# VectorE sums in place of a third matmul in 114 of 384 first-layer units, with in-place squares and later lags

## The chip, the cores and the metric

One core of a Trainium2 chip. The metric is the device time of one execution, in microseconds, as the median over several executions. All executions quoted here ran in the fast state; the time before the change varied from 652.4 to 655.0 us over all its runs. Ratios are the mean time of one kernel's fast runs over that of the other's of the same rounds, so not quite the ratio of the medians that are quoted.

Engine names in the profile: PE is TensorE, PEld its weight loads, DVE is VectorE, ACT is ScalarE, POOL is GpSimd. Two memories occur in the code: SBUF holds the kernel's tiles, and PSUM takes the results of matmuls. A *bank* is here one PSUM tile of 128 x 512 fp32 values; the kernel keeps six that the transforms and the first layer share, and two for the second layer. The *granted clock* is the share of TensorE's full clock that the profile records.

## The reference, cut to what matters

```python
# x: (8, 3008, 256), w_in: (256, 2048), w_out: (2048, 256), all float32
X = np.fft.fft(np.fft.fft(x, axis=1), axis=2).real
X = X.reshape(24064, 256)
h = np.maximum(X @ w_in, 0.0)
out = h * h @ w_out
```

The kernel computes the sequence transform as four real transforms per sequence, folds the transform along the features into the first layer's weights, and uses the symmetry of the result. Rows k and S-k of the output ("a pair") share their transforms: one is a sum, the other a difference of the same products. There are 8 x 1505 = 12040 pairs.

## The kernel before: the parts that the change touches

Pairs are worked in 25 chunks, mostly of 512 pairs. A *unit* is one chunk times 128 of the 2048 hidden features, so a full chunk has 16 units. The main loop takes one unit per *step*. With P and Q the transformed data of a sequence, and G1, G2 the folded weights, a unit needs

- relu(G1 P + G2 Q) for rows k ("s half"),
- relu(G1 P - G2 Q + an edge term) for rows S-k ("d half").

The kernel before makes both in one PSUM bank, with three matmuls of 512 columns. G3 is -2 G2, but 0 in the edge row (the last of Q's 128 rows), which enters both halves with the same sign.

```python
    def x_front(c, u):                       # two matmuls, relu of the s half
        ...
            for sn, G in ((0, G1), (1, G2)):
                for (b, i, o, l) in segs:
                    mm(xb[:, j, o : o + l], G[:, fs], PQ[b][sn][:, i : i + l], ...)
        act(r_of(c, u, 0), xb, AF.Relu)                          # L575
        return (c, u, xb)

    def x_back(cur):                         # third matmul, relu of the d half
        ...
                mm(xb[:, j, o : o + l], G3[:, fs], PQ[b][1][:, i : i + l], False, True)
        act(r_of(c, u, 1)[:, :, ::-1], xb, AF.Relu)              # L585

    def x_square(cur):                       # once per two units
        ...
            vt(h2, r, r, op=ALU.mult)                            # L599
```

The second layer of a chunk (128 matmuls of 256 columns, with 128x128 blocks of h as weights) is spread over the steps of the next chunk. This loop sets the order in which every engine gets its instructions:

```python
    for si, (c, u) in enumerate(steps):
        left = NFC // chunks[c][2] - u
        take = [mmq.pop(0) for _ in range(-(-len(mmq) // left))]   # second-layer matmuls
        cur = x_front(c, u)
        h = len(take) // 2
        posts = [f() for f in take[:h]]
        if prev is not None:
            x_back(prev)
        posts += [f() for f in take[h:]]
        ...
        if prev is not None:
            x_square(prev)
            if prev[0] != c:
                mmq += mm2_ops(prev[0])
        prev = cur
        for f in side.get(si, []):           # transforms of later sequences
            f()
```

So the third matmul of a unit comes one step after its first two, and the square in the same step as the relu that it needs.

## Time and profile before

| | before |
|---|---|
| median of 3 runs | 654.32 us (652.42 to 654.83) |
| profiled span | 651.9 us |
| TensorE, ACT, VectorE busy | 629.8, 511.7, 355.5 us |
| a full chunk, start to start | about 24.4 us, or 25 to 28 with transforms |

The head of the profile page (span, then busy time, share of the span and number of instructions of each engine), and the two lines of its chain of waits:

```profile
span 651.9 us, 11930 instructions
...
PE 629.8 (97%) x4834; PEld 459.5 (70%) x4834; DVE 355.5 (55%) x518; ACT 511.7 (78%) x934; POOL 49.4 (8%) x66
...
PE 92%; DVE 4%; DMA 1%; ACT 1%; issue 0%; POOL 0%; DVEq 0%; ACTq 0%; POOLq 0%
PE po L72 50%; PE xb L72 36%; PE pf L72 6%; DMA x<-in_x_dram,idx 1%; DVE h L599 1%; DVE u L329 1%; DVE wout L660 0%; DVE v L341 0%; ACT r L585 0%; ACT r L575 0%; DVE tm L235 0%; DVE qt L422 0%; ACT os L533 0%; DVE tt L182 0%; ACT G L308 0%
```

The chain says who is to be made shorter: TensorE, with the second layer (po) and the first (xb). Busy time alone would not say so, since matmuls overlap and their ends are modelled. TensorE's rate is read from start to start in the timeline of the kernel before (start, duration, engine, line, operation, output and inputs):

```profile
433.33 0.38 PE L72 MATMUL xb<-pt,G 128*128 128x512 f16 x1
433.55 0.38 PE L72 MATMUL xb<-qt,G 128*128 128x512 f16 x1
433.76 0.60 PE L72 MATMUL po<-wout,h 128*128 128x256 f16 x4
434.20 0.38 PE L72 MATMUL xb<-qt,G 128*128 128x512 f16 x1
```

A matmul "takes" 0.38 us, but the next one starts 0.22 us later; four of 256 columns take 0.44 us. One engine lies idle a great deal, as the waits list of the kernel before shows (who waited for whom: total us, times, longest):

```profile
DVE h L599 <- ACT r L585: 250.8, 164, 3.5
...
PE po L72 <- DVE h L599: 3.5, 2, 2.4
...
PE xb L72 <- ACT r L575: 2.5, 4, 0.9
```

VectorE's squares wait 250 us for ACT's relus, and nobody minds: TensorE waits for a square twice. These waits tell where there is room for more work. What an instruction costs is in the groups by shape of the kernel before (count | busy us, mean ns | idle before and its releaser):

```profile
L599 DVE TENSOR_TENSOR h<-r 128x2048 f16<-128x2048 f16 x184 | 225.2, 1224 | 250.8 <-ACT r L585 250.8
L585 ACT ACTIVATE r<-xb 128x512 f16<-128x512 f32 x368 | 222.0, 603 | 17.2 <-PE xb L72 1.3
...
L329 DVE TENSOR_TENSOR u<-x 127x765 f16<-127x765 f32 x32 | 29.0, 948 | 0.3 <-DMA x<-in_x_dram,idx 0.3
...
L425 DVE TENSOR_TENSOR pt<-as,pf 128x377 f16<-128x377 f32 x8 | 4.4, 548 | 4.1 <-PE pf L72 4.0
```

### The profile page before, as it was taken

The page shows a single profiled execution, that of the slowest core. Times are in us where ns is not written, and L with a number is a line of the kernel's source. Part 1 is how long each engine was busy: PE and PEld are TensorE (multiplying, and loading weights), DVE is VectorE, ACT ScalarE, POOL GpSimd, SP SyncE. Part 2 cuts the span into 40 slices and gives each one's busy share as a digit, 9 for nine tenths or more (in the row PEclk, how much of TensorE's full clock was granted, in tenths as well). Part 3 has the DMA queues.
Part 4 walks back from the last instruction along what each step waited for, and adds up shares of the span by engine and source line. Part 5 has one row for each costly group of instructions (what it writes and reads, how often), then busy time and mean ns, then how long its engine had stood idle before and what let it go on. Part 6 is the DMA issues. An engine that isn't in the chain of part 4 may idle for free.

```text
span 651.9 us, 11930 instructions
## 1 busy us (share of the span) xinstructions
PE 629.8 (97%) x4834; PEld 459.5 (70%) x4834; DVE 355.5 (55%) x518; ACT 511.7 (78%) x934; POOL 49.4 (8%) x66
## 2 busy tenths in 40 slices
PE   3889999999999999999999999999999999999997
PEld 1566677666776777767777668777787677877786
DVE  8878787694764447544674444444334444434331
ACT  5867888777888788788887778887887878888872
POOL 8103023030200004000000000000000000000000
PEclk9989999999999999999999999999999999999999
DMA  8935484572641018111111111111111110111112
GB/s 274 298 85 131 110 210 124 159 180 97 158 115 50 33 44 217 57 38 50 33 49 33 49 34 40 42 45 39 49 34 49 33 49 33 50 37 46 49 50 67
DMA packets 33758, 54.47 MB, mean 84 GB/s; under 512 B 4446, under 2 KB 28562, under 8 KB 33702
## 3 DMA queue, kind: packets, MB, share of 16 engines
q0 software_dynamic: 6256, 27.45, 16.0%
q1 hardware_dynamic: 27398, 26.22, 12.4%
q8 instruction: 38, 0.62, 0.4%
q14 instruction: 18, 0.15, 0.1%
q10 hardware_dynamic: 48, 0.02, 0.0%
HBM read 29.02 MB, written 24.64 MB: 82 GB/s over the span
## 4 chain that ended last, share of the span: by engine, by line
PE 92%; DVE 4%; DMA 1%; ACT 1%; issue 0%; POOL 0%; DVEq 0%; ACTq 0%; POOLq 0%
PE po L72 50%; PE xb L72 36%; PE pf L72 6%; DMA x<-in_x_dram,idx 1%; DVE h L599 1%; DVE u L329 1%; DVE wout L660 0%; DVE v L341 0%; ACT r L585 0%; ACT r L575 0%; DVE tm L235 0%; DVE qt L422 0%; ACT os L533 0%; DVE tt L182 0%; ACT G L308 0%
## 5 line engine op out<-in xcount | busy, mean ns | idle before, releaser
L72 PE MATMUL po<-wout,h 128*128 128x256 f16 x3024 | 445.7, 273 | 3.5 <-DVE h L599 3.5
L72 PEld LDWEIGHTS <-h 128*128 128x128 f16 x3024 | 286.0, 98 | 122.3 <-DVE h L599 4.4
L599 DVE TENSOR_TENSOR h<-r 128x2048 f16<-128x2048 f16 x184 | 225.2, 1224 | 250.8 <-ACT r L585 250.8
L575 ACT ACTIVATE r<-xb 128x512 f16<-128x512 f32 (+1 forms) x384 | 227.8, 593 | 91.2 <-PE xb L72 88.6
L72 PE MATMUL xb<-qt,G 128*128 128x512 f16 (+16 forms) x1024 | 286.5, 323 | 3.8 <-ACT r L575 2.5
L585 ACT ACTIVATE r<-xb 128x512 f16<-128x512 f32 (+1 forms) x384 | 228.2, 594 | 19.0 <-PE xb L72 2.5
L72 PEld LDWEIGHTS <-G 128*128 128x128 f16 x1536 | 144.5, 98 | 41.7 <-issue 7.4
L72 PE MATMUL xb<-pt,G 128*128 128x512 f16 (+16 forms) x512 | 146.8, 324 | 0.0
L533 ACT ACTIVATE os<-po 128x512 f32<-128x512 f32 x94 | 55.7, 592 | 6.3 <-PE po L72 6.2
L329 DVE TENSOR_TENSOR u<-x 127x765 f16<-127x765 f32 x32 | 29.0, 948 | 0.3 <-DMA x<-in_x_dram,idx 0.3
L100 POOL DMA_INDIRECT x<-in_x_dram,idx x18 | 25.0, 1389 | 5.4 <-issue 4.8
L72 PEld LDWEIGHTS <-w 127*128 127x128 f16 (+1 forms) x192 | 21.5, 118 | 5.3 <-DVE w L347 1.0
L393 ACT ACTIVATE as<-pf 128x377 f32<-128x377 f32 (+5 forms) x32 | 15.5, 484 | 9.8 <-PE pf L72 9.7
L123 POOL DMA_DIRECT2D x<-in_x_dram x14 | 7.9, 562 | 198.3 <-DVE u L333 198.1
L72 PE MATMUL pf<-sinT,w 127*127 127x377 f16 (+1 forms) x96 | 20.7, 323 | 0.0
L72 PE MATMUL pf<-cosT,w 127*128 127x377 f16 (+1 forms) x96 | 20.0, 323 | 0.1
L347 DVE TENSOR_TENSOR w<-v 127x381 f16<-127x381 f16 x64 | 19.7, 353 | 0.0
L72 PE MATMUL warm<-ez 128*128 128x512 f16 x18 | 6.3, 520 | 10.9 <-DVE ez L622 10.9
L341 DVE TENSOR_TENSOR v<-u 127x768 f16<-127x768 f16 x32 | 16.5, 552 | 0.3
L72 PEld LDWEIGHTS <-ez 127*128 127x128 f16 (+1 forms) x42 | 4.5, 110 | 15.2 <-DVE ez L622 10.9
L603 DVE TENSOR_TENSOR h<-r 128x528 f16<-128x528 f16 (+2 forms) x24 | 7.5, 339 | 11.2 <-ACT r L585 9.3
L425 DVE TENSOR_TENSOR pt<-as,pf 128x377 f16<-128x377 f32 (+1 forms) x16 | 8.8, 549 | 8.6 <-PE pf L72 7.5
(95 smaller groups left out, 123.6 us busy)
## 6 DMA issues: line engine op xcount, KB each, us to landing
out_dram<-os SPq DMA_DIRECT2D x157, 128.0 KB
x<-in_x_dram POOLq DMA_DIRECT2D x14, 756.0 KB, 10.1
wst<-in_moe_w_in_dram POOLq DMA_DIRECT2D x4, 512.0 KB, 6.6
wot<-in_moe_w_out_dram POOLq DMA_DIRECT2D x1, 2048.0 KB, 14.4
x<-in_x_dram SPq DMA_DIRECT2D x2, 756.0 KB
x<-in_x_dram,idx POOLq DMA_INDIRECT x18, 11.5
x<-in_x_dram POOLq DMA_DIRECT2D x14, 2.0 KB, 12.1
out_dram<-os SPq DMA_DIRECT2D x2, 108.0 KB
```

Of the source, the lines that this page charges most:

```text
L72: nc.tensor.matmul(o, l, r, start=start, stop=stop, skip_group_check=True)
L100: nc.gpsimd.indirect_dma_start(out=x4[0:NP, 2 + s, q : q + rows, :].rearrange("p q d -> p (q d)"), out_offset=None, in_=bass.AP(tensor=x.t ...
L123: nc.gpsimd.dma_start(out=x4[0:NP, s, :, :], in_=up(b, s))
L329: return lambda: vt(u[k, s, q0 : q0 + NQ // 2, 1:D], x4[k, s, q0 : q0 + NQ // 2, 1:D], x4[k, 3 - s, ::-1, :][:, q0 : q0 + NQ // 2, D - 1 : ...
L341: vt(vs[s][k, qs, :], u[k, 0, qs, :], u[k, 1, qs, :], op=ALU.subtract if s else ALU.add)
L347: return lambda: vt(w[k, i, q : q + 3, 0 : P - 1], vs[s][k, q : q + 3, 1:P], vs[s][k, q : q + 3, D - 1 : P : -1], op=ALU.add if i < 2 else ...
L393: act(st["a"][0:m, :], st[0][0:m, :], AF.Copy, bias=0.0, scale=1.0 if fin[0] is None else fin[0])
L425: vt(lo_, a, bp, op=ALU.add)
L533: act(os_, po, AF.Copy, bias=0.0, scale=HS * HS)
L575: act(r_of(c, u, 0), xb, AF.Relu)
L585: act(r_of(c, u, 1)[:, :, ::-1], xb, AF.Relu)
L599: vt(h2, r, r, op=ALU.mult)
```

## The change

The intent: TensorE binds and VectorE idles, so let VectorE make the sum and the difference. In a *split unit* G2 Q and G1 P go to two banks of their own (two matmuls, not three); ACT copies the first to SBUF; VectorE computes 2 g e - G2 Q (e is the edge row of Q, broadcast to all partitions, and g its weights) and then both clamped sums, which are the relus. 114 of the 384 units are split: 2 of 16 in chunks 3 to 5, 5 of 16 in chunks 6 to 14, 7 of 16 in chunks 15 to 23.

Further: relus write straight into the tile that the second layer reads and are squared in place, in a ring of 19 tiles of two units; one of eight squares of chunks 6 to 23 goes to ACT; back matmuls come two steps after the front (LAG), squares one step later still (SQ), and the second layer of a chunk starts at step 3 of the next chunk instead of step 1. The plans for folding later inputs are stretched, and two weight loads are cut in four to fit the ring. The diff, cut to its core:

```diff
+    YZ = [(0, 0)] * 3 + [(2, 0)] * 3 + [(5, 1)] * 9 + [(7, 1)] * 9 + [(0, 0)]
+    # y of 16 units split, z of 8 squares on ACT; u is split where (u * y + 8) % 16 < y
...
-    rp = ctx.enter_context(tc.tile_pool(name="rp", bufs=3))
-    h2p = ctx.enter_context(tc.tile_pool(name="h2p", bufs=2))
+    h2p = ctx.enter_context(tc.tile_pool(name="h2p", bufs=19))
...
+    def e_spread(c):     # the edge row, broadcast to all partitions; issued three steps ahead
+        ...
+            nc.gpsimd.dma_start(out=ebc[c][:, o : o + l], in_=PQ[b][1][P - 1 : P, ...])
+    def x_split(c, u):
+        xs = [psx.tile([P, 512], F32, name=nm, tag="x")[:, 0:n] for nm in ("xo", "xe")]
+        for t, G, sn in ((xs[0], G2, 1), (xs[1], G1, 0)):
+            for (b, i, o, l) in segs:
+                mm(t[:, o : o + l], G[:, fs], PQ[b][sn][:, i : i + l], o == 0, True)
+        bs = tgp.tile([P, 2, CH], F32, name="bs", tag=("tt", "tm")[nsplit[0] % 2])
+        act(bs[0], xs[0], AF.Copy, bias=0.0, scale=1.0)                                # L629
+        def add():
+            stt(out=bs[1], in0=ebc[c][:, 0:n], scalar=gE2[:, u : u + 1], in1=bs[0],
+                op0=ALU.mult, op1=ALU.subtract)                                        # L632
+            def sat(o, t):
+                nc.vector._custom_dve(TENSOR_ADD_SAT, out=o, in0=xs[1], in1=t, s0=BIG, s1=0.0)  # L636
+            sat(r_s(c, u)[:, 0, :], bs[0])
+            relu_d(c, u, lambda o, i: sat(o[:, 0, :], bs[1]))
+        return (c, u, None, add)
...
+        if u // 2 in PLAN[c][1]:
+            act(h2[:, 0:nf], h2[:, 0:nf], AF.Square)                                   # L660
+            rest.append(lambda: act(h2[:, nf:], h2[:, nf:], AF.Square))                # L661
             return
+        vt(h2, h2, h2, op=ALU.mult)                                                    # L663
...
+    LAG = 2
+    SQ = 1
     for si, (c, u) in enumerate(steps):
+        while wait:                          # chunks whose last square was in an earlier step
+            d = wait.pop(0)
+            mmq += mm2_ops(d)
+            due = si + NFC // chunks[d + 1][2]
...
+        flight.append((x_split if u in PLAN[c][0] else x_front)(c, u))
...
+        if len(flight) > LAG:
+            x_back(flight[0])
+            made.append(flight.pop(0))
...
+        if len(made) > SQ:
+            retire()                         # square; after a chunk's last: wait.append(chunk)
+        if len(flight) > 1 and flight[-2][3]:
+            flight[-2][3]()                  # VectorE's sums of the unit of the step before
```

In the changed kernel the relu of the s half is L605 and that of the d half L651.

More of the change, by code (lines that the diff above doesn't have):

```diff
@@ L8 @@
 from concourse._compat import with_exitstack
+from concourse.dve_ops import TENSOR_ADD_SAT
 F32 = mybir.dt.float32
@@ L19 @@
 R23 = float(2.0 ** 23)
+BIG = 3.0e38
 @with_exitstack
@@ L133 @@
     wout16 = const.tile([P, NFC, D], F16, name="wout16")
-    wst = h2p.tile([P, 2, F], F32, name="wst", tag="h2")
-    wot = h2p.tile([P, NFC, D], F32, name="wot", tag="h2")
+    wst = [h2p.tile([P, 2, F // 4], F32, name="wst", tag="h2") for _ in range(4)]
+    wot = [h2p.tile([P, NFC // 4, D], F32, name="wot", tag="h2") for _ in range(4)]
     wS = 2.0 * math.pi / S
@@ L296, in gcast @@
     def gcast(c, cp):
-        cp(win16(c), wst[:, :, c * 512 : (c + 1) * 512])
+        cp(win16(c), wst[c])
     def gmat(c):
@@ L480, with plan, e_weights, e_double @@
         g += n
-    h2t = {}
-    def h2v(c):
-        n = chunks[c][1]
-        return h2t[c][:, 0 : NFC * 2 * n].rearrange("p (f t) -> p f t", f=NFC)
+    YZ = [(0, 0)] * 3 + [(2, 0)] * 3 + [(5, 1)] * 9 + [(7, 1)] * 9 + [(0, 0)]
+    def plan(c, y, z):
+        if chunks[c][1] != CH:
+            return (), ()
+        return ([u for u in range(NFC) if (u * y + 8) % NFC < y],
+                [p for p in range(NFC // 2) if (p * z + 4) % (NFC // 2) < z])
+    PLAN = [plan(c, *YZ[c]) for c in range(len(chunks))]
+    gE = const.tile([P, NFC], F16, name="gE")
+    gE2 = const.tile([P, NFC], F32, name="gE2")
+    def e_weights():
+        for f in range(NFC):
+            nc.sync.dma_start(out=gE[:, f : f + 1], in_=G2[P - 1 : P, f * P : (f + 1) * P])
+    def e_double():
+        ts(out=gE2, in0=gE, scalar1=2.0, scalar2=None, op0=ALU.mult)
+    h2t = {}
+    def h2v(c, u):
+        n, nf = chunks[c][1:3]
+        if (c, u // 2) not in h2t:
+            t = h2p.tile([P, 4 * CH], F16, name="h2", tag="h2")
+            h2t[c, u // 2] = t[:, 0 : 4 * nf * n].rearrange("p (f t) -> p f t", f=2 * nf)
+        return h2t[c, u // 2]
     def mm2_ops(c):
@@ L544, in f @@
                 w = 2 * m if s == 2 else m
-                mm(st["o"][0:w, j, :], h2v(c)[:, fc, o : o + w], wout16[:, fc, :],
+                mm(st["o"][0:w, j, :], h2v(c, fc // nf)[:, fc % (2 * nf), o : o + w], wout16[:, fc, :],
                    fc == 0 and j == 0, fc == NFC - 1)
@@ L553, in mm2_ops, with relu_d, r_s @@
         return ops
-    rt = {}
-    def r_of(c, u, s):
-        g0, n, nf, segs = chunks[c]
-        if u % 2 == 0 and s == 0:
-            t = rp.tile([P, 4 * CH], F16, name="r", tag="r")
-            rt[c, u // 2] = t[:, 0 : 4 * nf * n].rearrange("p (f s n) -> p f s n", f=2 * nf, s=2)
-        o = u % 2 * nf
-        return rt[c, u // 2][:, o : o + nf, s, :]
+    def relu_d(c, u, put):
+        n, nf = chunks[c][1:3]
+        o = u % 2 * nf
+        d = h2v(c, u)[:, o : o + nf, n : 2 * n]
+        k = n % P
+        if k:
+            put(d[:, :, 0:k][:, :, ::-1], slice(0, k))
+            put(d[:, :, k:n][:, :, ::-1], slice(k, n))
+        else:
+            put(d[:, :, ::-1], slice(0, n))
+    def r_s(c, u):
+        n, nf = chunks[c][1:3]
+        o = u % 2 * nf
+        return h2v(c, u)[:, o : o + nf, 0:n]
     def x_front(c, u):
@@ L574, in x_front @@
                        j == 0 and sn == 0 and o == 0, sn == 1)
-        act(r_of(c, u, 0), xb, AF.Relu)
-        return (c, u, xb)
+        act(r_s(c, u), xb, AF.Relu)
+        return (c, u, xb, None)
+    ebc = {}
+    def e_spread(c):
+        g0, n, nf, segs = chunks[c]
+        ebc[c] = esp.tile([P, CH], F16, name="eb", tag="eb", bufs=2)
+        for (b, i, o, l) in segs:
+            nc.gpsimd.dma_start(out=ebc[c][:, o : o + l],
+                              in_=PQ[b][1][P - 1 : P, i : i + l].unsqueeze(1).to_broadcast([1, P, l]))
+    nsplit = [0]
+    def x_split(c, u):
+        g0, n, nf, segs = chunks[c]
+        fs = slice(u * P, (u + 1) * P)
+        xs = [psx.tile([P, 512], F32, name=nm, tag="x")[:, 0:n] for nm in ("xo", "xe")]
+        for t, G, sn in ((xs[0], G2, 1), (xs[1], G1, 0)):
+            for (b, i, o, l) in segs:
+                mm(t[:, o : o + l], G[:, fs], PQ[b][sn][:, i : i + l], o == 0, True)
+        nsplit[0] += 1
+        bs = tgp.tile([P, 2, CH], F32, name="bs", tag=("tt", "tm")[nsplit[0] % 2])
+        bs = [bs[:, j, 0:n] for j in range(2)]
+        act(bs[0], xs[0], AF.Copy, bias=0.0, scale=1.0)
+        def add():
+            stt(out=bs[1], in0=ebc[c][:, 0:n], scalar=gE2[:, u : u + 1], in1=bs[0], op0=ALU.mult,
+                op1=ALU.subtract)
+            def sat(o, t):
[3 more added lines that the diff above has]
+        return (c, u, None, add)
     def x_back(cur):
-        c, u, xb = cur
+        c, u, xb = cur[:3]
+        if xb is None:
+            return
         g0, n, nf, segs = chunks[c]
@@ L584, in x_back @@
                 mm(xb[:, j, o : o + l], G3[:, fs], PQ[b][1][:, i : i + l], False, True)
-        act(r_of(c, u, 1)[:, :, ::-1], xb, AF.Relu)
+        relu_d(c, u, lambda o, i: act(o, xb[:, :, i], AF.Relu))
     def x_square(cur):
-        c, u, _ = cur
-        nf = chunks[c][2]
+        c, u = cur[:2]
         if u % 2 == 0:
             return
-        if u == 1:
-            h2t[c] = h2p.tile([P, NFC * 2 * CH], F16, name="h2", tag="h2")
-        r = rt.pop((c, u // 2))
-        n = chunks[c][1]
-        h2 = h2v(c)[:, (u - 1) * nf : (u + 1) * nf]
-        if n % P == 0:
-            h2 = h2.rearrange("p f (s n) -> p f s n", s=2)
-            vt(h2, r, r, op=ALU.mult)
+        h2 = h2v(c, u)
+        if u // 2 in PLAN[c][1]:
+            nf = chunks[c][2]
+            act(h2[:, 0:nf], h2[:, 0:nf], AF.Square)
+            rest.append(lambda: act(h2[:, nf:], h2[:, nf:], AF.Square))
             return
-        full = n // P * P
-        for s, i, l, o in ((0, 0, n, 0), (1, full, n - full, n), (1, 0, full, 2 * n - full)):
-            vt(h2[:, :, o : o + l], r[:, :, s, i : i + l], r[:, :, s, i : i + l], op=ALU.mult)
+        vt(h2, h2, h2, op=ALU.mult)
     alloc_pq(0)
@@ L611 @@
         cs = slice(c * F // 4, (c + 1) * F // 4)
-        nc.gpsimd.dma_start(out=wst[:, :, cs],
+        nc.gpsimd.dma_start(out=wst[c],
                           in_=moe_w_in[:, cs].rearrange("(c p) f -> p c f", p=P))
-    nc.gpsimd.dma_start(out=wot, in_=moe_w_out.rearrange("(c p) o -> p c o", p=P))
+    for c in range(4):
+        nc.gpsimd.dma_start(
+            out=wot[c], in_=moe_w_out[c * F // 4 : (c + 1) * F // 4, :].rearrange(
+                "(c p) o -> p c o", p=P))
     for h in range(2):
@@ L659, in wcast @@
         cs = slice(c * NFC // 4, (c + 1) * NFC // 4)
-        nc.vector.tensor_copy(wout16[:, cs, :], wot[:, cs, :])
+        nc.vector.tensor_copy(wout16[:, cs, :], wot[c])
     spread([(lambda c=c: wcast(c)) for c in range(4)], 3, 7)
@@ L668 @@
     spread(stage1_ops(0, 1, True), 11, 15)
-    FOLD = {0: [(1, 0.5, 0.66)], 1: [(2, 0.02, 0.2), (3, 0.38, 0.56), (4, 0.7, 0.85)],
-            2: [(5, 0.1, 0.4)], 3: [(6, 0.1, 0.4)], 4: [(7, 0.1, 0.4)]}
+    FOLD = {0: [(1, 0.5, 0.66)], 1: [(2, 0.02, 0.28), (3, 0.3, 0.56), (4, 0.58, 0.85)],
+            2: [(5, 0.06, 0.96)], 3: [(6, 0.04, 0.96)], 4: [(7, 0.04, 0.85)]}
     ST1 = {0: (0.66, 0.98)}
@@ L686, with retire @@
             side.setdefault(at(0.4), []).append(lambda bb=b + 1: e_row(bb))
-    prev = None
-    mmq = []
-    for si, (c, u) in enumerate(steps):
-        left = NFC // chunks[c][2] - u
-        take = [mmq.pop(0) for _ in range(-(-len(mmq) // left))]
-        cur = x_front(c, u)
+    side.setdefault(7, []).append(e_weights)
+    side.setdefault(20, []).append(e_double)
+    for si, (c, u) in enumerate(steps):
+        if u == 0 and PLAN[c][0]:
+            side.setdefault(si - 3, []).append(lambda c=c: e_spread(c))
+    LAG = 2
+    SQ = 1
+    flight = []
+    made = []
+    rest = []
+    mmq = []
+    wait = []
+    due = 0
+    def retire():
+        v = made.pop(0)
+        x_square(v)
+        if v[1] == NFC // chunks[v[0]][2] - 1:
+            wait.append(v[0])
+    for si, (c, u) in enumerate(steps):
+        while wait:
+            d = wait.pop(0)
+            mmq += mm2_ops(d)
+            due = si + NFC // chunks[d + 1][2]
+        take = [mmq.pop(0) for _ in range(-(-len(mmq) // max(1, due - si)))]
+        flight.append((x_split if u in PLAN[c][0] else x_front)(c, u))
         h = len(take) // 2
         posts = [f() for f in take[:h]]
-        if prev is not None:
-            x_back(prev)
+        if len(flight) > LAG:
+            x_back(flight[0])
+            made.append(flight.pop(0))
         posts += [f() for f in take[h:]]
@@ L701 @@
                 p()
-        if prev is not None:
-            x_square(prev)
-            if prev[0] != c:
-                mmq += mm2_ops(prev[0])
-        prev = cur
+        while rest:
+            rest.pop()()
+        if len(made) > SQ:
+            retire()
+        if len(flight) > 1 and flight[-2][3]:
+            flight[-2][3]()
         for f in side.get(si, []):
             f()
-    x_back(prev)
-    x_square(prev)
-    mmq += mm2_ops(prev[0])
+    if flight[-1][3]:
+        flight[-1][3]()
+    while flight:
+        x_back(flight[0])
+        made.append(flight.pop(0))
+        while made:
+            retire()
+    while rest:
+        rest.pop()()
+    for d in wait:
+        mmq += mm2_ops(d)
     for f in mmq:
```

## The prediction

> **What bounds it now: TensorE.** The busy table has PE at 97% of a 651.9 us span, ACT 78%, DVE 55%; the windows table has PE busy all of every window from 80 to 580 us, at a granted clock of 1.00. The chain of waits is 92% PE (second-layer products 50%, first-layer 36%). In the timeline near 400 us a 512-column matmul starts 0.22 us after the one before, a 256-column one 0.11 us. A full chunk is 48 first-layer and 128 second-layer matmuls, 10.5 + 14.1 = 24.6 us, plus 1.3 for the transform.
>
> **Removed.** The plan drops the third matmul in 2 units of each of 3 chunks, 5 of each of 9, 7 of each of 9: 114 of 384 units. 114 x 0.2195 us = 25.0 us of PE, all on the critical path. ACT loses one 0.60 us eviction per such unit (two relus become one copy): 68 us.
>
> **Added on VectorE per such unit.** One scalar_tensor_tensor and two saturating adds on 128x512 fp32. In the groups by shape a 377-element fp32 tensor_tensor takes 549 ns, a 765-element one 948: about 1.03 ns an element. [...] Estimate: 0.69 us for an add, 0.74 for the scalar_tensor_tensor (377 elements: 606 ns), 0.08 less back to back: 1.9 us a unit, 213 us in all. One of eight squares moves to ACT in 18 chunks (1.22 us off DVE, about 2.1 on ACT, from the 1.05 us 1024-element cast). DVE goes from 355 to about 545 us busy.
>
> In a chunk with 7 units DVE needs about 13.2 + 8.0 + 1.3 = 22.5 us against PE's 24.4, ACT about 20. So PE still binds, with DVE at 92%.
>
> **Moved.** Back matmuls come two steps later, squares one more, second-layer matmuls run from step 4 of the next chunk. A split unit takes two of six PSUM banks; counting allocations, a bank is reused at least three steps (4.5 us) after it was taken, mostly four, while a normal unit now holds its bank over two. So I expect short PE waits, no stall chain. The 19-granule ring reuses a granule about three steps after its last reader.
>
> At the start the second layer begins some 3 steps later, while ACT binds there: about 2 us lost. At the end, leftovers of chunk 23 cover the last squares' latency: about 2 us won (PE waited 2.4 us there).
>
> **Prediction: 654.3 - 25.0 + about 1.5 of friction = 631 us, range 625 to 639. Faster by over 2%: 0.88; within 2%: 0.10; slower: 0.02.**
>
> **What would show it.** 114 third matmuls gone; PE still 96-98% of the span and most of the chain; DVE busy 530-560 us, in the last third 9 tenths; ACT 460-490 us; saturating adds at 0.65-0.75 us; PE's waits for VectorE under 5 us in all. If PE waits on xe or xo banks repeatedly, the margin argument is wrong.
>
> **What would make it wrong.** The custom add costing over 0.85 us: VectorE then binds the nine late chunks, and 5-15 us come back. Bank reuse tighter than counted, so each backlog on VectorE stops PE. The edge row's broadcasts landing late, behind the loads of x: VectorE, then PE, would wait at each chunk's start. An ACT square costing more than twice 1.05 us. Upside: fewer stalls at the start, 627.

0.69 us is 549 + 135 x 1.03 ns, from the groups by shape of the kernel before.

## The result, and the profile after

| | before | after |
|---|---|---|
| median | 653.37 us (4 runs) | 630.25 us (4 runs, 629.46 to 630.93) |
| profiled span | 651.9 | 628.5 |
| TensorE busy | 629.8 | 606.4 |
| VectorE busy | 355.5 | 536.8 |
| ACT busy | 511.7 | 479.3 |

The ratio is 0.9644, 95% interval 0.9618 to 0.9669. The result is correct. The head and the chain of the profile page after:

```profile
span 628.5 us, 11983 instructions
...
PE 606.4 (96%) x4682; PEld 446.9 (71%) x4682; DVE 536.8 (85%) x827; ACT 479.3 (76%) x872; POOL 68.8 (11%) x97
...
PE 92%; DVE 6%; ACT 1%; issue 0%; DVEq 0%; POOL 0%; POOLq 0%; ACTq 0%
PE po L73 52%; PE xb L73 25%; PE pf L73 6%; PE xo L73 4%; PE xe L73 4%; DVE h L663 2%; PE warm L73 1%; DVE u L330 1%; DVE v L342 0%; DVE w L348 0%; DVE wout L723 0%; DVE tm L248 0%; ACT h L605 0%; DVE tm L236 0%; DVE tt L183 0%
```

TensorE still makes up 92% of the chain, now with xb, xo and xe at 33% together in place of 36%. The waits list after has, for TensorE, nothing but the following lines after the initial warm-up, and none of them lies later than 90 us:

```profile
PE xb L73 <- ACT h L605: 4.1, 5, 1.8
PE pf L73 <- DVE cosT L279: 2.0, 2, 1.1
PE xb L73 <- DVE qt L423: 0.7, 1, 0.7
PE xb L73 <- DVE qt L424: 0.2, 1, 0.2
```

So 180 us more of work on VectorE cost TensorE no wait at all. What the new instructions cost, from the groups by shape after:

```profile
L663 DVE TENSOR_TENSOR h<-h 128x2048 f16<-128x2048 f16 x166 | 202.2, 1218 | 29.7 <-ACT h L651 27.0 <-DVE w L348 0.2
...
L636 DVE CUSTOM_DVE_ANT_0 h<-xe,bs 128x512 f16<-128x512 f32 x228 | 145.9, 680 | 0.0
...
L632 DVE SCALAR_TENSOR_TENSOR bs<-eb,gE,bs 128x512 f32<-128x512 f16 x114 | 85.0, 745 | 9.1 <-ACT bs L629 8.4 <-ACT h L605 0.7
L629 ACT ACTIVATE bs<-xo 128x512 f32<-128x512 f32 x114 | 68.5, 601 | 21.0 <-PE xo L73 16.3 <-ACT h L605 1.3
...
L661 ACT ACTIVATE h<-h 128x1024 f16<-128x1024 f16 x18 | 19.1, 1064 | 0.0
```

The squares' idle time before them fell from 250.8 to 29.7 us: that is where the sums went. The VectorE timeline after, in a chunk with seven split units, shows how full it is:

```profile
451.70 1.23 DVE L663 TENSOR_TENSOR h<-h 128x2048 f16<-128x2048 f16 x1
452.85 0.75 DVE L632 SCALAR_TENSOR_TENSOR bs<-eb,gE,bs 128x512 f32<-128x512 f16 x1
453.51 1.28 DVE L636 CUSTOM_DVE_ANT_0 h<-xe,bs 128x512 f16<-128x512 f32 x2
454.89 1.23 DVE L663 TENSOR_TENSOR h<-h 128x2048 f16<-128x2048 f16 x1
```

The sums take 0.66 + 1.2 us from start to start and the square 1.15: together with a gap 3.2 us for the two steps that one square covers.

Where the 23.4 us of the profiled spans came from can be read from the starts of the chunks (each chunk's first matmul with G1, found by counting in the two traces):

| stretch | before | after | difference |
|---|---|---|---|
| start to chunk 4 | 102.4 | 100.5 | -1.9 |
| chunks 4 and 5 (2 split) | 55.3 | 54.5 | -0.4 each |
| chunks 6 to 14 (5 split) | 233.9 | 224.4 | between -0.9 and -1.1 each |
| chunks 15 to 23 (7 split) | 227.4 | 213.7 | -1.5 each |
| chunk 24 to the last matmul | 29.0 | 31.4 | +2.3 |
| last matmul to the end | 3.8 | 4.0 | +0.2 |

The chunks 4 to 23 hold 112 split units and lost 24.1 us together, 0.215 us for each matmul left out. Nothing else shows in them. The first and the last stretch mirror each other: at chunk 4, 24 second-layer matmuls that the kernel before has done are still to come (24 x 0.11 = 2.6 us), and they come back at the end.

### The profile page after: what moved, and what is told of

Same layout as the page of the kernel before. It is cut to its first block, busy times and chain, and to the rows that moved or that the text cites. A ratio compares the mean times of both kernels' runs of the same rounds, so it can differ in the third digit from the quotient of the medians.

```text
span 628.5 us, 11983 instructions
## 1 busy us (share of the span) xinstructions
PE 606.4 (96%) x4682; PEld 446.9 (71%) x4682; DVE 536.8 (85%) x827; ACT 479.3 (76%) x872; POOL 68.8 (11%) x97
## 4 chain that ended last, share of the span: by engine, by line
PE 92%; DVE 6%; ACT 1%; issue 0%; DVEq 0%; POOL 0%; POOLq 0%; ACTq 0%
PE po L73 52%; PE xb L73 25%; PE pf L73 6%; PE xo L73 4%; PE xe L73 4%; DVE h L663 2%; PE warm L73 1%; DVE u L330 1%; DVE v L342 0%; DVE w L348 0%; DVE wout L723 0%; DVE tm L248 0%; ACT h L605 0%; DVE tm L236 0%; DVE tt L183 0%
## 5 line engine op out<-in xcount | busy, mean ns | idle before, releaser
L663 DVE TENSOR_TENSOR h<-h 128x2048 f16<-128x2048 f16 (+1 forms) x174 | 207.8, 1195 | 41.1 <-ACT h L651 36.5
L605 ACT ACTIVATE h<-xb 128x512 f16<-128x512 f32 (+1 forms) x270 | 159.2, 590 | 67.8 <-PE xb L73 67.1
L73 PE MATMUL xb<-qt,G 128*128 128x512 f16 (+11 forms) x720 | 203.6, 322 | 4.9 <-ACT h L605 4.1
L651 ACT ACTIVATE h<-xb 128x512 f16<-128x512 f32 (+2 forms) x286 | 160.4, 567 | 20.3 <-PE xb L73 13.9
L636 DVE CUSTOM_DVE_ANT_0 h<-xe,bs 128x512 f16<-128x512 f32 x228 | 145.9, 680 | 0.0
L73 PE MATMUL xb<-pt,G 128*128 128x512 f16 (+9 forms) x360 | 103.8, 324 | 0.3 <-DVE qt L424 0.2
L632 DVE SCALAR_TENSOR_TENSOR bs<-eb,gE,bs 128x512 f32<-128x512 f16 x114 | 85.0, 745 | 9.1 <-ACT bs L629 8.4
L629 ACT ACTIVATE bs<-xo 128x512 f32<-128x512 f32 x114 | 68.5, 601 | 21.0 <-PE xo L73 16.3
L73 PE MATMUL xo<-qt,G 128*128 128x512 f16 (+14 forms) x152 | 43.4, 327 | 0.0
L73 PE MATMUL xe<-pt,G 128*128 128x512 f16 (+14 forms) x152 | 43.4, 326 | 0.0
L330 DVE TENSOR_TENSOR u<-x 127x765 f16<-127x765 f32 x32 | 29.7, 945 | 0.0
```

The costliest lines, as they stand in the source:

```text
L73: nc.tensor.matmul(o, l, r, start=start, stop=stop, skip_group_check=True)
L330: return lambda: vt(u[k, s, q0 : q0 + NQ // 2, 1:D], x4[k, s, q0 : q0 + NQ // 2, 1:D], x4[k, 3 - s, ::-1, :][:, q0 : q0 + NQ // 2, D - 1 : ...
L605: act(r_s(c, u), xb, AF.Relu)
L629: act(bs[0], xs[0], AF.Copy, bias=0.0, scale=1.0)
L632: stt(out=bs[1], in0=ebc[c][:, 0:n], scalar=gE2[:, u : u + 1], in1=bs[0], op0=ALU.mult, op1=ALU.subtract)
L636: nc.vector._custom_dve(TENSOR_ADD_SAT, out=o, in0=xs[1], in1=t, s0=BIG, s1=0.0)
```

## The experiments

Twelve runs were made, in three groups; each group shared a chip and the runs of the kernel before. All but the first give correct results. Only the third group has the changed kernel itself on the same chip; elsewhere compare with it by the ratios.

Theory A: TensorE binds throughout, the gain is the time of the matmuls left out, and everything else in the change moves little. Rival B: part of the gain comes from the lags and the ring. Rival C: VectorE's added work has already taken part of the possible gain.

### Only the matmul left out

The kernel before, with the third matmul dropped in the same 114 units. Its output is wrong, which doesn't matter for the time.

```diff
-        for j in range(nf):
+        for j in range(nf if (u * YZ[c] + 8) % NFC >= YZ[c] else 0):     # YZ: 2, 5, 7 of 16
             fs = slice((u * nf + j) * P, (u * nf + j + 1) * P)
             for (b, i, o, l) in segs:
                 mm(xb[:, j, o : o + l], G3[:, fs], PQ[b][1][:, i : i + l], False, True)
```

> Kernel before, with the third matmul left out in the same 114 units and nothing else changed (a wrong result on purpose). Theory A, the gain is the TensorE time of the dropped matmuls and nothing else: 114 x 0.215 us = 24.5 us less, about 629 us, so VectorE's added work costs the change next to nothing. Theory B, part of the gain comes from the lags and the ring: this run gains clearly less, 12 to 20 us (634 to 641). Theory C, VectorE's work already takes some of the gain: this run is clearly faster than the changed kernel, 620 to 626.

Measured: 630.72 us, ratio 0.9635 (0.9613 to 0.9657). This is what leaving these matmuls out gives by itself, and the changed kernel (630.25, ratio 0.9644) stands at the same place within the intervals. VectorE's 180 us of added work cost nothing that these runs resolve (about 2 us). Rivals B and C both fall in the form given: no more than that is gained or lost beyond the matmuls.

### The lags and the ring without split units

```diff
-    YZ = [(0, 0)] * 3 + [(2, 0)] * 3 + [(5, 1)] * 9 + [(7, 1)] * 9 + [(0, 0)]
+    YZ = [(0, 0)] * 25
```

> The changed kernel with its plan emptied: ring, in-place squares and later lags only. Theory A: no gain, 652 to 656 us, about 2 us lost at the start to the later second layer and about 1 won at the end. Theory B: 640 to 648 us.

Measured: 654.12 us, ratio 1.0009 (0.9985 to 1.0032). The ring, the in-place squares and the lags by themselves are worth nothing.

### The old lags with split units

```diff
-    LAG = 2
-    SQ = 1
+    LAG = 1
+    SQ = 0
...
             made.append(flight.pop(0))
+            if made[-1][3]:
+                made[-1][3]()               # the sums, just before the square
...
-        if len(flight) > 1 and flight[-2][3]:
-            flight[-2][3]()
```

> The changed kernel with the lags set back (back matmuls one step later, not two; squares at once; the vector sums just before the square). If the lags are what lets TensorE not wait for VectorE, the last granule's square comes about as late as its first reader: 0.5 to 1.5 us of TensorE waits in each of 18 chunks, 636 to 648 us, and waits of second-layer matmuls for the square in the list. If they are not needed: 628 to 631 us, with the 2 us of the start won back.

Measured: 653.76 us, ratio 0.9993 (0.9976 to 1.0011). The expectation's direction held and its size was far off: not a part, but the *whole* gain is gone. The same 114 matmuls are left out, but TensorE now waits. The chain line of its profile page shows the shift, from 92% TensorE to 55%:

```profile
PE 55%; DVE 32%; ACT 9%; issue 4%; DVEq 0%; ACTq 0%; POOL 0%; POOLq 0%
```

and its waits list has what was not there before:

```profile
DVE h L663 <- ACT h L651: 68.7, 46, 3.9
...
PE xb L73 <- ACT h L605: 17.9, 22, 1.5
...
ACT h L660 <- DVE h L636: 16.0, 14, 1.9
...
PEld L73 <- DVE h L663: 11.2, 18, 1.3
...
PE po L73 <- DVE h L663: 5.9, 11, 1.0
```

After 90 us, where the changed kernel has no wait of TensorE, two lines are left for it, 19.4 of the 23.5 us by which the profiled spans differ:

```profile
PE xb L73 <- ACT h L605: 13.9, 17, 1.3
PE po L73 <- DVE h L663: 5.5, 10, 1.0
```

So split units without the lags give nothing, and the lags without split units give nothing; only both together give 23 us. My prediction had treated the lags as something moved that would cost or win a microsecond or two. The second group of runs asks which lag it is.

### Nine split units in the last nine chunks

```diff
-    YZ = ... + [(7, 1)] * 9 + [(0, 0)]
+    YZ = ... + [(9, 1)] * 9 + [(0, 0)]
```

> Nine split units in place of seven in each of the last nine chunks. Theory A with VectorE near its limit: per chunk VectorE needs 9 x 1.9 + 7 x 1.15 + 1.3 (transform) = 26.4 us against TensorE's 23.8, so VectorE binds there: 2 us lost per chunk in place of 0.4 won, 643 to 655 us in all, VectorE busy over 97% there, TensorE waiting for banks. A rival that only counts TensorE: 18 x 0.215 = 3.9 us won, 626 us.

Measured: 648.60 us, ratio 0.992 (0.990 to 0.994), inside the range given. The windows table of this run, late in the kernel (busy us and count of TensorE, weight loads, VectorE, ACT, GpSimd; granted clock, DMA):

```profile
430.00:480.00 50.00, 46.77 (x369) 35.28 (x367) 49.62 (x70) 30.18 (x56) 1.60 (x3) 1.00 0.31 48
```

against the same window of the changed kernel:

```profile
430.00:480.00 50.00, 50.00 (x411) 39.35 (x409) 47.76 (x64) 38.86 (x68) 2.14 (x4) 1.00 0.36 52
```

VectorE at 49.6 of 50 us now binds, and TensorE gets through 369 matmuls instead of 411. Two more split units a chunk turn a gain of 24 us into one of 6. Seven was close to the most that VectorE holds.

### Only the square's lag set back

```diff
     LAG = 2
-    SQ = 1
+    SQ = 0
```

> The changed kernel with only the square's lag set back (back matmuls still two steps later). With both lags set back the whole gain was lost, with about 18 us of TensorE waits for relu evictions and as much for squares in the list. If the back matmul's lag is what counts (P): most of the gain stays, 630 to 638 us. If the square's lag counts (S)[...]: 643 to 654 us.

Measured: 640.31 us, ratio 0.9808 (0.9786 to 0.983). Between the two ranges: 11 us of the gain are lost.

### Only the back matmul's lag set back

```diff
-    LAG = 2
+    LAG = 1
...
-        if len(flight) > 1 and flight[-2][3]:
-            flight[-2][3]()
+        if made and made[-1][3]:
+            made[-1][3]()                   # the same unit and the same place as before
```

> The counterpart: back matmuls one step later as before, the square's lag of one kept. P: 643 to 654 us, with TensorE waiting for relu evictions before the back matmul. S: 630 to 638 us. If both are about equal parts, this and the run before lie near 640 each.

Measured: 628.47 us, ratio 0.9633 (0.961 to 0.9655). The second step of back lag buys nothing. Theory P falls, S holds in direction. This run and the one before it are a good pair: in both the square stands two steps behind its unit's first matmuls, and in both the second layer starts at step 2 of the next chunk. They differ in whether a square stands in the same step as the relu that it reads (640.3) or one step later (628.5). From the waits lists between 90 and 590 us, the run with squares at once has

```profile
DVE h L663 <- ACT h L651: 47.4, 42, 3.7
...
ACT h L660 <- DVE h L636: 12.5, 13, 1.6
...
PEld L73 <- DVE h L663: 10.4, 14, 1.7
...
PE po L73 <- DVE h L663: 6.5, 11, 1.5
```

and the run with one step between them

```profile
DVE h L663 <- ACT h L651: 31.9, 33, 2.9
...
ACT h L660 <- DVE h L636: 0.3, 1, 0.3
```

with no wait of TensorE for a square at all.

### All squares on VectorE

```diff
-    YZ = [(0, 0)] * 3 + [(2, 0)] * 3 + [(5, 1)] * 9 + [(7, 1)] * 9 + [(0, 0)]
+    YZ = [(0, 0)] * 3 + [(2, 0)] * 3 + [(5, 0)] * 9 + [(7, 0)] * 9 + [(0, 0)]
```

> The changed kernel with no square on ACT: all back on VectorE, 18 x 1.15 us more there, 18 x 2.1 us less on ACT. By the sum VectorE then needs 7 x 1.86 + 8 x 1.15 + 1.3 = 23.5 us a late chunk against TensorE's 24.1: still under it, so at most 2 us lost, 629 to 633 us. If VectorE has less room than the sum says: 636 us or more, VectorE busy over 97% late.

Measured: 629.48 us, ratio 0.9645 (0.9624 to 0.9665). No loss: VectorE is busy 98.1 of 100 us in its window from 400 to 500, and TensorE still 100.0. Moving squares to ACT was not needed at seven split units.

### More split units

```diff
-    YZ = ... + [(5, 1)] * 9 + [(7, 1)] * 9 + [(0, 0)]
+    YZ = ... + [(6, 1)] * 9 + [(8, 2)] * 9 + [(0, 0)]
```

> Six split units in each of the nine middle chunks and eight in each of the nine late ones, where two of eight squares go to ACT. VectorE 8 x 1.86 + 6 x 1.15 + 1.3 = 23.1 us late against TensorE's 23.9, ACT about 21: TensorE still binds, 18 x 0.215 = 3.9 us less, 625 to 628 us. If the two staging buffers or the banks bind first, as in the run with nine: 632 us or more.

Measured: 633.62 us, ratio 0.97 (0.9678 to 0.9723). Slower than the changed kernel, but not for either of the reasons expected. By the chunk starts, eight of the nine middle chunks are 0.21 or 0.22 us shorter, exactly one matmul; the late ones differ by -0.22 to +0.44, so at eight there is no more to win. One single chunk, number 10, is 6.25 us *longer*. The VectorE timeline of this run has the reason:

```profile
255.34 1.22 DVE L663 TENSOR_TENSOR h<-h 128x2048 f16<-128x2048 f16 x1
261.56 0.75 DVE L632 SCALAR_TENSOR_TENSOR bs<-eb,gE,bs 128x512 f32<-128x512 f16 x1 [5.00 <-DMA eb<-qt]
```

VectorE stands still for 5.0 us for the broadcast of the edge row. The GpSimd timeline shows a part of why it is late: the queue had been held by loads of x, one of which waited for VectorE until 248.81 us, and the broadcast was issued only at 251.84. That is not the whole reason, since the changed kernel issued the same broadcast at 251.22 and did not wait: there VectorE came to it at 258.66, here it was free for it at 256.56, and here the transfer took 9.6 us to land. Why it took so long stays open. In the control run below, the changed kernel too waits for such a broadcast once, 1.1 us on VectorE. In the run with more split units TensorE then waited 3.8 us for a bank, and its mean granted clock in the window from 240 to 320 us is 0.96, where it is 1.00 in the changed kernel.

### A version from these results

The back lag undone, six split units in the middle chunks (seven late, as in the changed kernel), and the broadcast issued eight steps ahead where the chunk lies in one sequence. A first form, with eight steps for all chunks, read an edge row before it was written. The sums are issued as in the run with only the back lag undone; that part of the edit is left out here.

```diff
-    YZ = ... + [(5, 1)] * 9 + [(7, 1)] * 9 + [(0, 0)]
+    YZ = ... + [(6, 1)] * 9 + [(7, 1)] * 9 + [(0, 0)]
...
-            side.setdefault(si - 3, []).append(lambda c=c: e_spread(c))
+            side.setdefault(si - (3 if len(chunks[c][3]) > 1 else 8), []).append(lambda c=c: e_spread(c))
...
-    LAG = 2
+    LAG = 1
```

> The changed kernel with back matmuls one step later again (the square's lag kept), six split units in place of five in the nine middle chunks, and the edge row's broadcast issued eight steps ahead, not three, in chunks that lie in one sequence. TensorE has nine matmuls less, 9 x 0.215 = 1.9 us, and a start as in the run with the back lag undone (628.5): 626 to 627.5 us, 0.3 to 0.6% under the changed kernel of the same chip. If the late broadcast of the run with more splits still stops VectorE once: 630 to 634 us.

Measured: 625.85 us, ratio 0.9574 (0.9554 to 0.9594), 625.28 to 627.56 in five runs: just below the range expected, and VectorE waits for no broadcast. The control, the changed kernel unmodified on the same chip:

> The changed kernel, unmodified, as control on this chip: 628.5 to 631 us by every theory; TensorE's granted clock below 1.00 in part of the first 50 us in some executions.

Measured: 629.50 us, ratio 0.9623 (0.9602 to 0.9643), 628.01 to 630.50 in five runs. The two intervals do not meet, so this version beats both kernels, by 3.65 us of medians against the changed one. Where it comes from can be read from the chunk starts of its profile against the control's: 1.9 us at the start (chunk 4 begins at 97.9 us, against 99.9), 1.6 in the nine middle chunks (nine matmuls of 0.215 us would be 1.9), 1.3 after the start of chunk 24, and 0.4 lost in the late chunks. The mean granted clock of its profiled run is 0.999, against 0.997 in the control's, see below. Three things were changed at once, and only the back lag was also run alone.

### Squares at once, second layer later

Does the square's lag matter because the first second-layer matmuls come too soon behind the last square (R), or because a square that waits for ACT keeps VectorE idle (O; above, 47.4 us of such waits with squares at once and 31.9 with one step between)? This run keeps squares at once (SQ = 0) but starts each chunk's second layer one step later.

```diff
-            wait.append(v[0])
+            wait.append((v[0], si + 2))       # the run before it in effect: si + 1
...
-        while wait:
-            d = wait.pop(0)
+        while wait and wait[0][1] <= si:
+            d = wait.pop(0)[0]
```

> As the run with squares at once (640.3 us), with the second layer of each chunk started one step later, so that its first readers stand as far behind the last square as in the changed kernel. Theory R, the lag matters because the first second-layer matmuls come too soon after the last square: 628 to 632 us. Theory O, it matters because a square right behind its relu stops VectorE[...] until ACT is there, and the lost room is felt everywhere: 637 to 641 us. Between: both.

Measured: 633.80 us, ratio 0.9692 (0.9672 to 0.9712). Of the 11 us lost with squares at once, about 6.5 come back (by medians across two chips; by the ratios 7.6 of 12.1). After 90 us TensorE had waited 7.5 us for squares; these waits are gone, and 2.0 us of others are there. So R has the larger share; that the rest is O is an inference.

The same for both lags set back (second layer at step 3, as in the changed kernel, not at step 1; in the edit above, si + 3):

> As the run with both lags set back (653.8 us), with the second layer started two steps later, at the step at which it starts in the changed kernel. Theory R: 628 to 635 us. Theory O: 645 to 654 us, VectorE's waits for ACT's evictions and TensorE's for ACT's about as long as in that run (69 and 18 us).

Measured: 648.08 us, ratio 0.9904 (0.9882 to 0.9926). Here only 5.7 of 24.3 us come back (653.76 to 648.08 against 629.50), so O has the larger share. By the chunk starts seven of the nine late chunks each lose about 1.5 us against the changed kernel, which looks like one event a chunk. The timeline of this run shows one such event. The value in brackets is idle time and what ended it:

```profile
455.02 1.06 ACT L660 ACTIVATE h<-h 128x1024 f16<-128x1024 f16 x1 [0.79 <-DVE h L636]
...
456.60 0.75 DVE L632 SCALAR_TENSOR_TENSOR bs<-eb,gE,bs 128x512 f32<-128x512 f16 x1 [1.61 <-ACT bs L629]
...
456.94 1.06 ACT L661 ACTIVATE h<-h 128x1024 f16<-128x1024 f16 x1
...
457.89 0.60 ACT L605 ACTIVATE h<-xb 128x512 f16<-128x512 f32 x1
...
458.53 0.38 PE L73 MATMUL xb<-qt,G 128*128 128x512 f16 x1 [1.29 <-ACT h L605]
```

ACT stands at its square until VectorE's sums are there; VectorE then stands for 1.61 us for a copy that ACT has behind that square; the relu of the next unit comes last, and TensorE, which may add its third matmul to that bank only after that relu has read it, waits 1.29 us. In the waits list of this run TensorE's waits for such relus are 21.1 us in 20 times, and after 90 us they are all that is left:

```profile
PE xb L73 <- ACT h L605: 15.8, 14, 2.1
```

Each of these 14 comes within 3.6 us after a square on ACT that waited for VectorE's sums. In the run with both lags set back the same holds, within 5 us, for its 17 waits for relus (13.9 us); its 5.5 us of waits for squares, gone here, are about the 5.7 us that came back. In the event, ACT stood 0.79 us before its square and VectorE 1.61 us before its sum, and neither started anything behind the waiting instruction in that time. That the square on ACT is the cause in all these chunks is so read from the order of events in the traces, and not from a run without it. A run with both lags set back and all squares on VectorE would test it; it was not made, and this stays open.

The six runs on lags together:

| | back matmul, steps after front | square, steps after back | second layer starts at step | median us |
|---|---|---|---|---|
| changed kernel (control) | 2 | 1 | 3 | 629.50 |
| back lag undone | 1 | 1 | 2 | 628.47 |
| square at once | 2 | 0 | 2 | 640.31 |
| square at once, later reader | 2 | 0 | 3 | 633.80 |
| both set back | 1 | 0 | 1 | 653.76 |
| both set back, later reader | 1 | 0 | 3 | 648.08 |

The medians come from three chips; the kernel before had medians of 652.53 to 654.52 us on them.

## Why the prediction was right

**TensorE binds before and after.** Right: 97% and 96% of the span, 92% of the chain both times, no wait after 90 us in the changed kernel.

**25.0 us removed, all on the critical path.** Right, and slightly too much: 0.2195 us a matmul was taken from the timeline's two digits; the chunk starts give 24.1 / 112 = 0.215, so 24.5 us. The run that only drops the matmuls gives the same time as the change.

**Cost of the new operations.** Right: 680 ns for the clamped sum (mean of 228, half of them writing backwards; predicted 0.69), 745 for the scalar_tensor_tensor (0.74), 1.05 and 1.06 us for half a square on ACT, VectorE 536.8 us busy (545). The slope of 1.03 ns an element, read from fp32 tensor_tensors before the change (549 ns for 377 elements, 948 for 765), carried over to an add with two clamps: 688 ns by the slope, 680 in the run. From the scalar_tensor_tensor before (606 ns for 377 elements, PSUM and SBUF sources) to the new one (745 for 512, an f16 and an fp32 source, both in SBUF) it is 139 ns for 135 elements, the same slope.

**VectorE at 92%, so not over.** Right, and it was close: busy time late reads 94% (188.6 of 200 us from 380 to 580); seven fit (even with all squares on VectorE), eight win nothing, nine cost 18 us.

**Start and end, "about 2 us lost" and "about 2 us won".** Too large both. The premises, in the trace before: ACT is busy all of 24 to 32 us, and TensorE waited 2.5 us for its relus at the start; but the 2.4 us that TensorE waited for a square end at 39.08 us, at the start and not at the end. At chunk 4 the changed kernel is 1.9 us ahead, where two split units (0.4) and the 24 deferred matmuls (2.6) would make it 3.0: 1.1 us lost. At the end, +2.3 us stand against 2.6 deferred: 0.3 won. They nearly cancel, so the sum hid it. The "about 1.5 of friction" was not worked out term by term, and that it fits is luck: 0.5 too much for the matmuls, 1.1 lost at the start, 0.3 won and 0.2 lost at the end make 1.5. Much of what the start lost is clock: the windows from 40 to 44 and 44 to 48 us have a granted clock of 0.53 and 0.62 after, while before only those from 36 to 44 are below 1.00, at 0.88 and 0.69. That is an estimate of 3.4 against 1.7 us of lost full-speed time. In the control's profiled run the mean granted clock of the span is 0.997, as before the change, against 0.994 in the changed kernel's, and chunk 4 starts at 99.9 us, so about 0.7 of the 1.1. In windows of 0.8 us the two traces show one stretch each at a granted clock of 0.50, about 3.4 us long before (39.0 to 42.4 us) and 6.8 after (40.2 to 47.1). Each comes after windows with hardly any matmuls: none from 37.2 to 38.8 us before; none from 36.4 to 37.2 and one from 38.8 to 39.6 after. What sets the clock was not tested. The profiled runs of the version with only the back lag undone, and of the one built on it, have mean granted clocks of 1.000 and 0.999.

**Banks reused late enough.** Right in the result: TensorE waited for no xe or xo bank in the changed kernel. But it was the wrong thing to count on. What the margin really hangs on is that a square does not stand in the same step as the results that it reads. The prediction listed "squares one later" under what is moved, with no cost and no merit of its own; the runs show that with the old lags the whole gain is gone, and that of the two lags only the square's is needed. By the traces the larger part of that loss goes through ACT, whose squares stood waiting for VectorE's sums in front of the relus that TensorE needed. The result was right without this reason, and to that extent by luck.

**The edge row landing late.** Named as a risk; it does not stop the changed kernel, and it is what stopped the run with more split units, for 5.0 us.

## What to carry to other kernels

Work moved from the binding engine to one with idle time is free only if the receiving engine's waits were harmless and stay so: before, VectorE waited 250 us for ACT and nobody noticed; with the added sums (83% busy) the same order of instructions cost the whole gain. So when an engine fills up, put each of its instructions, and those of other engines that read its results, at least a step behind whatever it waits for, before judging the idea: here either half of the change alone was worth nothing. And to size such a move, weigh the worst chunk, not the average: VectorE's 85% over the span was 94% late, and two more units a chunk tipped it.
